# Batch 0's loads issued in one run, its tables built in waiting time, and the first odd product made in unit 5, in an FNet mixing and maxout feed-forward kernel

## The chip, the core and the metric

The kernel runs on one core of one Trainium2 chip. The metric is the device time of one execution in microseconds. The core has a matrix engine (PE, TensorE; its weight loads are listed apart as PEld), a vector engine (DVE), an activation engine (ACT), a general engine (POOL, GpSimd) and a queue engine that only issues transfers (SP). Each engine takes its own instructions strictly in the order in which the program wrote them; engines wait for one another through semaphores.

## The reference

The input `x` has 8 batches of 3072 tokens by 256 features. First comes a mixing step without weights: a discrete Fourier transform over the tokens and over the features, of which the real part is kept. Then each of the 24576 tokens goes through a feed-forward layer whose hidden value is the largest of three products:

```python
X = np.fft.fft(np.fft.fft(x, axis=1), axis=2).real      # 8 x 3072 x 256
t = X.reshape(24576, 256)
h = np.maximum(np.maximum(t @ w1, t @ w2), t @ w3)      # w1, w2, w3: 256 x 768
out = h @ w_out                                          # w_out: 768 x 256
```

Inputs and output are float32.

## The kernel before

**The mathematics.** The transform over the 3072 tokens is split as 24 x 128: stage `s` (class `Mix`, lines 440 to 456) multiplies by 24-point matrices `m24f` and `m24r`, and stage `k` (lines 460 to 476) by cosine and sine tables `tabs` with 13 rows of 128 angles, each row in three copies: sine, cosine and the sine's negative (`tab_minus`). The transform over the features is never applied to the tokens. It is multiplied into the weights once, at the start: `prep_first` and `prep_second` make `gE`, `gO`, `gD` (the features' table times w2 - w1 and w3 - w1, for the even and the odd part) and `gw` (the features' table times w1 times w_out). So the maximum becomes w1's part plus relu and maximum of two differences, and w1's part reaches the output through `gw` directly. Tokens r and 3072 - r share their even part and differ in the sign of the odd part; each token pair is therefore computed once as "plus" (`hp`) and once as "minus" (`hm`).

**The odd part once.** For one group of 128 token pairs (a slot; 12 slots to a batch), `l2_even` multiplies the even part by `gw` for two slots at a time, and ACT copies the result to `even`. `l2_odd` multiplies the odd part into a bank `po`; DVE forms `other = twice * scalar - po` (line 543) from it, where `twice` is a table that is made once from `gw`; POOL adds `other` to the even part (line 546) to get the minus half. The hidden products (`l2_hidden`, line 516: six for plus, six for minus) accumulate onto `po`. DVE adds `po` and the even lines into `ot` (line 570). The minus half is scattered to its rows by POOL (line 573), the plus half is stored by SP. There are two `po` banks, so a slot's odd product waits until `ot` of the slot two before it has been read from its bank.

**Order of the work.** The order is written out by hand; each engine's queue is the order of the program. A batch has three blocks of six units, 18 units in all. A unit on PE is four matmuls of 512 columns (`unit_plus`, lines 491 and 492), two for the minus side of the unit before (`unit_minus`, line 499), then some steps of a queue of hidden products of the block before (`l2_some`), then what a table `plan` has at that unit. The plan holds the next batch's transform (`s0` to `s6`, `k0` to `k5`), the loads of later batches on SP, and the casts (`turn_chunk`) by which POOL turns a loaded chunk of 32 or 33 rows into bf16, once forward (line 148) and once reversed (line 151). For batch 1 the casts stand in units 0, 2, 5 and 8 of batch 0, and stage `s0`, which reads all four chunks, in unit 10. Each PSUM bank of a unit is freed when ACT has taken its relu (`stmp`, line 505) and DVE its maximum (`hp` or `hm`, line 506) of the plus and the minus side; there are two banks of each kind, so unit n + 2 waits for both sides of unit n.

**The start.** POOL issues batch 0's first 112 rows as sixteen transfers that cast to bf16 on the way (`load_rows`, line 102), with iotas for the tables between them, and after them the weights. The weights' first half also releases batch 1's loads on SP. DVE makes the angles of the tables, ACT their sines; the angle rows 0 to 6 come first, then 7 to 12, then the 24-point matrices. PE runs 27 warming matmuls on `tab` (line 666), which read rows 0 and 1 of it and so wait for `tab_minus(0, 7)`. Then come batch 0's stages: `s0` to `s6`, half of the first weight product, `k0`, `k1`, the other half. In the units of block 0 follow four more pieces of `prep_first`, three of `prep_second` for `g1t` (line 404, one `pst` bank each), `gw` (line 413), and `twice` (line 422). Batch 0's rows 0 to 111 are turned and copied by ACT and DVE themselves (`turn_rows`, `lay_rows`, lines 133 and 325).

In block 1 of batch 0 the odd products are started ahead of time only when the even lines exist already. Otherwise `l2_block` makes them where they are needed:

```python
if (b, slot) not in odd:
    if (b, slot) not in lines:
        yield from l2_even(b, slot)
    l2_odd(b, slot)
```

Of the kernel before, what the change touches and what calls it, by code (L numbers as in the profile page):

```python
# [33 lines left out]
def kernel(  # L34
# [51 lines left out]
    mark = consts.tile([1, 1], FP32, tag="mark")  # L86
    two_row = consts.tile([128, 128], BF16, tag="two_row")
    sgn = consts.tile([128, 1], FP32, tag="sgn")
    dif = consts.tile([128, 1], FP32, tag="dif")
    twice = consts.tile([128, 256], FP32, tag="twice")  # L90
    t_mid = consts.tile([128, 2, B], BF16, tag="t_mid")
# [70 lines left out]
    def iota(t, pattern, base=0, cm=0):  # L162
        nc.gpsimd.iota(t, pattern, base=base, channel_multiplier=cm,
                       allow_small_or_imprecise_dtypes=True)
# [11 lines left out]
    iota(j128, [[1, 128]])  # L176
    i13 = gen.tile([128, 13], FP32, tag="i13")
    iota(i13, [[1, 13]])
# [3 lines left out]
    iota(jm24[:, 13:24], [[-1, 11]], base=-1)  # L182
    iota(jm24[:, 24:37], [[1, 13]])
    iota(jm24[:, 37:48], [[1, 11]], base=1)
    g24 = gen.tile([96, 5], FP32, tag="g24")
    iota(g24, [[24, 5]])
# [3 lines left out]
    iota(dvec[:, 2:4], [[64, 2]], base=32)  # L190
    load_rows(nc.gpsimd, x0v[:, 64:96, :], 0, 64, 96)
    load_rows(nc.gpsimd, x0v[:, 96:112, :], 0, 96, 112)

    first_half = None
    for jh in range(2):
# [4 lines left out]
        if jh == 0:  # L200
# [15 lines left out]
    for (name, value) in (("half_pi", 0.5 * math.pi), ("rnd", ROUND), ("n24", -24.0)):  # L216
# [4 lines left out]
    nc.vector.memset(two_row, 0.0)  # L221
    nc.vector.memset(two_row[0:1], 2.0)
    nc.vector.memset(gw[:, 512:513], 0.0)
    nc.vector.memset(gw[0:1, 512:513], 1.0)
    nc.vector.memset(m0f[:, 50:52], 0.0)
    nc.vector.memset(m0r[:, 50:52], 0.0)
    half = gen.tile([128, 256], FP32, tag="half")
    nc.vector.memset(half[:, 0:128], 64.0)
    nc.vector.memset(half[:, 128:256], 0.0)
# [4 lines left out]
    nc.vector.tensor_scalar(out=pi13, in0=i13, scalar1=pidx, scalar2=1.0 / 3072.0,  # L234
                            op0=ALU.mult, op1=ALU.mult)

    w = gen.tile([128, 13 * 128], FP32, tag="w")
    v = gen.tile([128, 13 * 128], FP32, tag="v")
    q = gen.tile([128, 13 * 128], FP32, tag="q")
    turn = 2.0 * math.pi  # L240

    def tab_angles(r0, r1):
        cs = slice(r0 * 128, r1 * 128)
        n = r1 - r0
        nc.vector.scalar_tensor_tensor(
            out=v[:, cs].rearrange("p (r j) -> p r j", j=128),
            in0=j128.unsqueeze(1).to_broadcast([128, n, 128]), scalar=p128,
            in1=pi13[:, r0:r1].unsqueeze(2).to_broadcast([128, n, 128]),
            op0=ALU.mult, op1=ALU.add)
        nc.vector.tensor_scalar(out=q[:, cs], in0=v[:, cs], scalar1=ROUND, scalar2=None,  # L250
                                op0=ALU.add)
        nc.vector.scalar_tensor_tensor(out=w[:, cs], in0=q[:, cs], scalar=-ROUND, in1=v[:, cs],
                                       op0=ALU.add, op1=ALU.subtract)

    def tab_sines(r0, r1):
        cs = slice(r0 * 128, r1 * 128)
        wr = w[:, cs].rearrange("p (r j) -> p r j", j=128)
        nc.scalar.activation(out=tabs[:, r0:r1, 0, :], in_=wr, func=AX.Sin, scale=-turn)
        nc.scalar.activation(out=w[:, cs], in_=w[:, cs], func=AX.Abs)
        nc.scalar.activation(out=tabs[:, r0:r1, 1, :], in_=wr, func=AX.Sin, scale=-turn,  # L260
                             bias=consts_of["half_pi"])

# [55 lines left out]
    def turn_rows(copy, r0, n, d0, d1):  # L318
        reverse(copy, xr0, x0_first[:, r0 * 64:(r0 + n) * 64], r0, n, d0, d1)
# [4 lines left out]
    def lay_rows(copy, xs, r0, n, d0=0, d1=33):  # L324
        copy(out=xn0[:, d0:d1, r0:r0 + n],
             in_=bass.AP(xs.tensor, xs.offset + d0, [xs.ap[0], [1, d1 - d0], [64, n]]))

    def bf_rows(r0, n):
# [8 lines left out]
    lay_rows(on_act, bf_rows(0, 32), 0, 32)  # L337
    lay_rows(on_dve, bf_rows(32, 32), 32, 32)

    turns = gen.tile([128, 256], BF16, tag="turns")  # L340
    nc.vector.memset(turns, 1.0)
    nc.vector.memset(turns.rearrange("p (q two g) -> p q two g", two=2, g=4)[:, :, 1, :], -1.0)
    vm = gen.tile([128, 256], FP32, tag="vm")
    qm = gen.tile([128, 256], FP32, tag="qm")
    nc.vector.scalar_tensor_tensor(
        out=vm.rearrange("p (k c) -> p k c", c=128),
        in0=dvec.unsqueeze(1).to_broadcast([128, 2, 128]), scalar=pidx,
        in1=half.rearrange("p (k c) -> p k c", c=128), op0=ALU.mult, op1=ALU.add)
    nc.vector.tensor_scalar(out=vm[:, 128:129], in0=pidx, scalar1=128.0, scalar2=64.0,
                            op0=ALU.mult, op1=ALU.add)  # L350
    nc.vector.tensor_scalar(out=qm, in0=vm, scalar1=256.0 * ROUND, scalar2=None, op0=ALU.add)
    nc.vector.scalar_tensor_tensor(out=vm, in0=qm, scalar=-256.0 * ROUND, in1=vm,
                                   op0=ALU.add, op1=ALU.subtract)
    nc.scalar.activation(out=md[0], in_=vm, func=AX.Sin, scale=float(-2.0 * math.pi / 256.0))
    turn_rows(on_act, 63, 32, 54, 65)
    turn_rows(on_dve, 63, 32, 32, 54)
    lay_rows(on_dve, bf_rows(64, 32), 64, 32)
    nc.vector.tensor_tensor(out=md[1], in0=md[0], in1=turns, op=ALU.mult)
    nc.vector.tensor_scalar(out=nmd_all, in0=md_all, scalar1=-1.0, scalar2=None, op0=ALU.mult)
    for (copy, a, b, c) in ((on_act, 49, 64, 17), (on_dve, 32, 49, 0)):  # L360
        turn_rows(copy, 95, 17, a, b)
        if copy is on_act:
            turn_rows(copy, 95, 16, 64, 65)
        lay_rows(copy, bf_rows(96, 16), 96, 16, c, c + 17 - c // 17)
    tab_minus(7, 13)
    nc.vector.tensor_scalar(out=sgn, in0=pidx, scalar1=0.0, scalar2=None, op0=ALU.is_equal)
# [297 lines left out]
    warm = ps_s.tile([128, 512], FP32, name="warm", tag="ps")  # L664
    for _ in range(27):
        nc.tensor.matmul(warm, tab[:, 0:128], tab[:, 0:512], start=True, stop=True)  # L666
    m = Mix(0)
    x0f = (lambda d: xn0[:, d, 0:128], rows_back(xr0))
    for k in range(7):
        m.s(k, x0f, pool=ps_s if k % 4 else ps_f,  # L670
            evict=nc.vector.tensor_copy if k in (1, 3, 5) else nc.scalar.copy)
    slots = [ps_s, ps_s, ps_f, ps_f]
    first = prep_first(0, lambda: slots.pop(0).tile([128, 512], FP32, name="psg", tag="ps"))
# [152 lines left out]
```

## Time and profile before

| | us |
|---|---|
| median of three runs | 422.15 (422.12 to 422.38) |
| the profiled execution | 422.23 |
| its span, first to last instruction | 420.3 |

Shares of the span: PE 94%, PEld 64%, DVE 74%, ACT 63%, POOL 76%. The granted clock of TensorE is recorded as full throughout. DMA moves 51.90 MB, a mean of 123 GB/s.

How to read the rows. In a row of the timeline the first number is the start in microseconds from the start of the span, the second is the time it took (for a row with x4, from the first start to the last end), then engine, line, operation, output from input and shapes. In brackets stands the idle time of the engine just before, and what ended it. A row of the waits reads "engine, what it was about to do, from whom it waited: microseconds in total, times, longest". Matmuls overlap in the rows: a 512-column matmul is shown with about 0.38 us, but the next one starts 0.22 us after it; a 256-column one has 0.27 us and 0.11 us.

### The profile page before, as it was taken

The numbers are of one execution on the slowest core, as the hardware profiler recorded it, in microseconds if no ns is written. First come the engines' busy times: TensorE is split into PE (matmuls) and PEld (weight loads), VectorE is DVE, ScalarE is ACT, GpSimd is POOL, SyncE is SP. The second block draws the span as 40 slices with busy tenths as digits, with TensorE's granted clock in tenths as the row PEclk, the third lists the DMA queues.
The fourth block names the chain that finished last, engine by engine and source line by source line (L and its number), as shares of the span: only waits on it lengthen the run. The fifth ranks groups of instructions, "written<-read, shape, count | busy, mean of one in ns | idle before, by whom it ended". The sixth has DMA issues, their size and how long they took to land.

```text
span 420.3 us, 9060 instructions
## 1 busy us (share of the span) xinstructions
PE 396.6 (94%) x3029; PEld 270.3 (64%) x3084; DVE 310.7 (74%) x558; ACT 263.3 (63%) x478; POOL 318.1 (76%) x431
## 2 busy tenths in 40 slices
PE   0898789999999999999999999999999999999996
PEld 0365457666776677667766676667766677666665
DVE  8868477677777877787767867787767877778884
ACT  6856546765676576656676566656676576655550
POOL 9927675999998888898887798898887844545551
PEclk9999999999999999999999999999999999999999
DMA  9999885386315863198314863177411222111314
GB/s 107 99 176 181 169 211 145 96 197 154 117 63 140 214 127 109 63 214 184 117 62 127 209 144 110 63 190 178 147 64 62 77 65 76 64 64 44 109 62 139
DMA packets 131174, 51.90 MB, mean 123 GB/s; under 512 B 113073, under 2 KB 128184, under 8 KB 131128
## 3 DMA queue, kind: packets, MB, share of 16 engines
q1 hardware_dynamic: 105408, 35.93, 35.6%
q0 software_dynamic: 24784, 15.08, 16.6%
q8 instruction: 24, 0.39, 0.4%
q10 hardware_dynamic: 936, 0.33, 0.3%
q14 instruction: 22, 0.18, 0.2%
HBM read 29.02 MB, written 25.17 MB: 129 GB/s over the span
## 4 chain that ended last, share of the span: by engine, by line
PE 91%; DVE 2%; ACT 2%; issue 2%; POOL 2%; DMA 1%; DVEq 0%; ACTq 0%; POOLq 0%
PE po L516 29%; PE pse L491 16%; PE pse L499 14%; PE pse L492 12%; PE ps L445 3%; PE ps L447 3%; PE po L540 3%; PE ps L473 2%; PE ps L471 2%; PE pl L529 2%; PE warm L666 2%; PE psg L385 1%; ACT stmp L505 1%; DMA out_dram<-ot 1%; POOL x L151 1%
## 5 line engine op out<-in xcount | busy, mean ns | idle before, releaser
L505 ACT ACTIVATE stmp<-pse 128x512 bf16<-128x512 f32 x288 | 171.4, 600 | 44.9 <-PE pse L492 29.0
L506 DVE TENSOR_TENSOR hp<-pse,stmp 128x512 bf16<-128x512 f32 x144 | 99.5, 691 | 92.5 <-ACT stmp L505 63.7
L573 POOL DMA_INDIRECT out_dram<-ot,rows_m x92 | 103.2, 1121 | 55.7 <-DVE ot L570 43.9
L491 PE MATMUL pse<-t,gE 128*128 128x512 bf16 x287 | 108.8, 379 | 2.2 <-ACT t L475 0.2
L506 DVE TENSOR_TENSOR hm<-pse,stmp 128x512 bf16<-128x512 f32 x144 | 99.1, 688 | 3.7 <-ACT stmp L505 3.5
L492 PE MATMUL pse<-t,gO 128*128 128x512 bf16 x250 | 94.6, 379 | 0.1
L516 PE MATMUL po<-wout_bf,hp 128*128 128x256 bf16 x576 | 85.9, 272 | 3.9 <-DVE other L543 3.9
L516 PE MATMUL po<-wout_bf,hm 128*128 128x256 bf16 x570 | 85.6, 273 | 0.2
L546 POOL TENSOR_TENSOR even<-even,other 128x256 f32<-128x256 f32 x92 | 66.4, 722 | 25.4 <-DVE other L543 22.9
L499 PE MATMUL pse<-t,gD 128*128 128x512 bf16 x272 | 82.2, 379 | 0.7
L516 PEld LDWEIGHTS <-hp 128*128 128x128 bf16 x576 | 56.3, 98 | 21.6 <-issue 6.6
L148 POOL CAST x<-xs 96x544 bf16<-96x544 f32 (+2 forms) x52 | 60.7, 1171 | 11.0 <-DMA xs<-in_x_dram 11.0
L516 PEld LDWEIGHTS <-hm 128*128 128x128 bf16 x576 | 56.3, 98 | 16.7
L570 DVE TENSOR_TENSOR ot<-po,even 128x512 f32<-128x512 f32 x92 | 62.8, 682 | 0.5 <-POOL even L546 0.3
L151 POOL CAST x<-xs 96x544 bf16<-96x544 f32 (+5 forms) x59 | 62.5, 1069 | 0.0
L475 ACT CAST t<-ps 128x512 bf16<-128x512 f32 x47 | 27.5, 585 | 38.2 <-PE ps L473 35.3
L499 PEld LDWEIGHTS <-gD 128*128 128x128 bf16 x288 | 27.9, 98 | 32.2
L452 ACT CAST z_all<-ps 128x480 bf16<-128x480 f32 x45 | 25.1, 558 | 36.9 <-PE ps L447 35.4
L543 DVE SCALAR_TENSOR_TENSOR other<-twice,po 128x256 f32<-128x256 f32 x92 | 43.8, 476 | 0.0
L492 PEld LDWEIGHTS <-gO 128*128 128x128 bf16 x288 | 28.1, 98 | 20.4 <-issue 1.7
L491 PEld LDWEIGHTS <-gE 128*128 128x128 bf16 x288 | 28.1, 98 | 20.3 <-issue 1.6
L532 ACT COPY even<-pl 128x512 f32<-128x512 f32 x46 | 27.0, 586 | 10.3 <-PE pl L529 9.8
(157 smaller groups left out, 379.7 us busy)
## 6 DMA issues: line engine op xcount, KB each, us to landing
xs<-in_x_dram SPq DMA_DIRECT2D x84, 198.0 KB
out_dram<-ot SPq DMA_DIRECT2D x90, 128.0 KB
xs<-in_x_dram SPq DMA_DIRECT2D x28, 192.0 KB
out_dram<-ot,rows_m POOLq DMA_INDIRECT x92
x<-in_x_dram POOLq DMA_DIRECT2D x12, 96.0 KB
w_bf<-in_moe_w_dram POOLq DMA_DIRECT2D x6, 192.0 KB
out_dram<-ot SPq DMA_DIRECT2D x17, 64.0 KB
xs<-in_x_dram SPq DMA_DIRECT2D x32, 5.8 KB
```

Of the source, the lines that this page charges most:

```text
L148: nc.gpsimd.tensor_copy(v[:, d0:d1, ch * 32:ch * 32 + 32], xs[:, 0:32 * 64].rearrange("p (bb dl) -> p dl bb", dl=64)[:, d0:d1, :])
L151: reverse(lambda out, in_: nc.gpsimd.tensor_copy(out, in_), v[:, 33:66, :], xs, ch * 32, 33 if ch == 3 else 32, 32 + d0, 32 + d1)
L491: nc.tensor.matmul(pse[:, 0:n], gE[i][:, js], te, start=True, stop=False)
L492: nc.tensor.matmul(pse[:, 0:n], gO[i][:, js], to, start=False, stop=True)
L499: nc.tensor.matmul(pse, gD[i][:, js], to, start=False, stop=True, skip_group_check=True)
L505: nc.scalar.activation(out=stmp[:, 0:n], in_=pses[0][:, 0:n], func=AX.Relu)
L506: nc.vector.tensor_tensor(out=dst, in0=src3, in1=stmp[:, 0:n], op=ALU.max)
L516: nc.tensor.matmul(po, hcols(jc), wout_bf[:, jc * 256:(jc + 1) * 256], start=False, stop=(jc == NJC - 1), skip_group_check=True)
L543: nc.vector.scalar_tensor_tensor(out=other, in0=twice, scalar=po[:, 256:257], in1=po[:, 0:256], op0=ALU.mult, op1=ALU.subtract)
L546: nc.gpsimd.tensor_tensor(out=line[:, 256:512], in0=line[:, 0:256], in1=other, op=ALU.add)
L570: nc.vector.tensor_tensor(out=ot, in0=po, in1=lin, op=ALU.add)
L573: stored(nc.gpsimd.indirect_dma_start(out, bass.IndirectOffsetOnAxis(ap=rows_m[0:128 - lo, b * 12 + slot: b * 12 + slot + 1], axis=0), ot[ ...
```

## The change

- **Loads.** The sixteen x loads of POOL follow each other directly. The iotas `i13`, `jm24`, `g24` and `dvec` are gone; DVE builds these small tables from `j128` with copies and scalar operations.
- **Tables.** The angle of row r and column j was computed for every row with three passes (product plus offset, rounding, difference). Now the rounded product `step` is formed once for 128 columns, and each row group takes two passes (offset minus `step`, then a correction by one where it exceeds a half). The rows come in groups 0 to 2, 3 to 6, 7 to 9 and 10 to 12. Only the first two groups stand ahead of the 24-point matrices; the passes of the other two stand between DVE's row copies, their sines between ACT's row copies, and the last sines (rows 10 to 12) after stage `s6`. `tab_minus(7, 13)` moves behind the stages too.
- **Features' table.** `vm` is made in two operations, its rounding stands behind DVE's last row copy, the sine `md[0]` behind stage `s2`'s copy on ACT, and `md[1]` and `nmd_all` behind `s3`'s copy on DVE (a copy and a negation of halves in place of a product with `turns`).
- **Memsets.** Those of `two_row` and of a column of `gw` move from DVE's start to POOL, behind the row numbers. Those of `half` and `turns` are gone.
- **Warming.** 35 matmuls in place of 27.
- **Last rows.** Of rows 96 to 111 DVE copies 22 of 33 columns reversed and 20 of 33 forward (17 and 17 before), ACT the others.
- **Weight products.** Of `prep_second`'s pieces two stand in unit 2 (one before), the third in unit 3, `gw` in unit 4, `twice` in unit 5. Behind it in unit 5 stands `l2_first`: the even lines of slots 0 and 1 and the odd product of slot 0. The branch in `l2_block` that made odd products where they are needed is gone.

Because slots 0 and 1 then have their even lines by unit 6, the order on the other engines changes with it. On POOL it was, in units 5 to 10: chunk 2's casts, slot 0's addition, slot 0's scatter, slot 1's addition, slot 2's addition, chunk 3's casts, the scatters of slots 1 and 2, slot 3's addition. After the change it is: slot 0's addition, chunk 2's casts, slot 1's addition, slot 0's scatter, slot 2's addition, slot 1's scatter, chunk 3's casts, slot 3's addition. From block 2 of batch 0 on, the order on all engines is the same as before. Cut to its core:

```diff
-    load_rows(nc.gpsimd, x0v[:, 0:32, :], 0, 0, 32)
-    jm24 = gen.tile([96, 48], FP32, tag="jm24")
-    iota(jm24[:, 0:13], [[1, 13]])
...
-    load_rows(nc.gpsimd, x0v[:, 32:64, :], 0, 32, 64)
-    dvec = gen.tile([128, 128], FP32, tag="dvec")
-    iota(dvec.rearrange("p (dl g) -> p dl g", g=4), [[1, 32], [64, 4]])
...
+    for r0 in (0, 32, 64):
+        load_rows(nc.gpsimd, x0v[:, r0:r0 + 32, :], 0, r0, r0 + 32)
     load_rows(nc.gpsimd, x0v[:, 96:112, :], 0, 96, 112)
...
     nc.gpsimd.tensor_copy(rows_m, rows_f)
+    nc.gpsimd.memset(two_row, 0.0)
+    nc.gpsimd.memset(two_row[0:1], 2.0)
+    nc.gpsimd.memset(gw[:, 512:513], 0.0)
+    nc.gpsimd.memset(gw[0:1, 512:513], 1.0)
...
+    nc.vector.tensor_scalar(out=step, in0=j128, scalar1=p128, scalar2=None, op0=ALU.mult)
+    nc.vector.tensor_scalar(out=near, in0=step, scalar1=ROUND, scalar2=None, op0=ALU.add)
+    nc.vector.scalar_tensor_tensor(out=step, in0=near, scalar=-ROUND, in1=step,
+                                   op0=ALU.add, op1=ALU.subtract)
...
     def tab_angles(r0, r1):
...
+        nc.vector.tensor_tensor(
+            out=wr.rearrange("p (r j) -> p r j", j=128),
+            in0=pi13[:, r0:r1].unsqueeze(2).to_broadcast([128, n, 128]),
+            in1=step.unsqueeze(1).to_broadcast([128, n, 128]), op=ALU.subtract)
+        nc.vector.scalar_tensor_tensor(out=wr, in0=wr, scalar=0.5, in1=wr,
+                                       op0=ALU.is_gt, op1=ALU.subtract)
...
-    tab_angles(0, 7)
-    tab_sines(0, 7)
-    tab_angles(7, 13)
-    tab_sines(7, 13)
+    for (r0, r1) in ((0, 3), (3, 7)):
+        tab_angles(r0, r1)
+        tab_sines(r0, r1)
...
     turn_rows(on_act, 0, 31, 32, 65)
+    tab_angles(7, 10)
+    tab_angles(10, 13)
+    lay_rows(on_act, bf_rows(0, 32), 0, 32)
+    tab_sines(7, 10, (0, 1))
     turn_rows(on_dve, 31, 32, 32, 65)
...
-            if (b, slot) not in odd:
-                if (b, slot) not in lines:
-                    yield from l2_even(b, slot)
-                l2_odd(b, slot)
...
-    for _ in range(27):
+    for _ in range(35):
         nc.tensor.matmul(warm, tab[:, 0:128], tab[:, 0:512], start=True, stop=True)
...
     for k in range(7):
         m.s(k, x0f, pool=ps_s if k % 4 else ps_f,
             evict=nc.vector.tensor_copy if k in (1, 3, 5) else nc.scalar.copy)
+        if k == 2:
+            nc.scalar.activation(out=md[0], in_=vm, func=AX.Sin, scale=float(-2.0 * math.pi / 256.0))
+        if k == 3:
...
+    tab_sines(10, 13, (1, 2))
+    tab_minus(7, 13)
...
+    def l2_first():
+        for _ in l2_even(0, 0):
+            pass
+        l2_odd(0, 0)
+
     for (u, fn) in ((0, prep_some), (0, prep_some), (1, prep_some), (1, prep_some),
-                    (2, lambda: m.k(2)), (2, prep_some), (3, lambda: m.k(3)),
-                    (3, prep_some), (4, prep_some), (5, prep_some), (5, prep_some),
+                    (2, lambda: m.k(2)), (2, prep_some), (2, prep_some),
+                    (3, lambda: m.k(3)), (3, prep_some), (4, prep_some),
+                    (5, prep_some), (5, l2_first),
                     (6, lambda: m.k(4)), (7, lambda: m.k(5)), (7, m.end),
```

More of the change, by code (lines that the diff above doesn't have):

```diff
@@ L233 @@
     pi13 = gen.tile([128, 13], FP32, tag="pi13")
-    nc.vector.tensor_scalar(out=pi13, in0=i13, scalar1=pidx, scalar2=1.0 / 3072.0,
+    nc.vector.tensor_scalar(out=pi13, in0=j128[:, 0:13], scalar1=pidx, scalar2=1.0 / 3072.0,
                             op0=ALU.mult, op1=ALU.mult)
-    w = gen.tile([128, 13 * 128], FP32, tag="w")
-    v = gen.tile([128, 13 * 128], FP32, tag="v")
-    q = gen.tile([128, 13 * 128], FP32, tag="q")
+    step = gen.tile([128, 128], FP32, tag="step")
+    near = gen.tile([128, 128], FP32, tag="near")
@@ L242, in tab_angles @@
     def tab_angles(r0, r1):
-        cs = slice(r0 * 128, r1 * 128)
+        wr = rows_of(r0, r1)
         n = r1 - r0
[L245 to L251, printed above, removed]
@@ new lines, in tab_angles, with tab_sines @@
+        nc.vector.scalar_tensor_tensor(out=wr, in0=wr, scalar=0.5, in1=wr,
+                                       op0=ALU.is_gt, op1=ALU.subtract)
+    def tab_sines(r0, r1, parts=(0, 1, 2)):
+        wf = rows_of(r0, r1)
+        wr = wf.rearrange("p (r j) -> p r j", j=128)
+        if 0 in parts:
+            nc.scalar.activation(out=tabs[:, r0:r1, 0, :], in_=wr, func=AX.Sin, scale=-turn)
+        if 1 in parts:
+            nc.scalar.activation(out=wf, in_=wf, func=AX.Abs)
+        if 2 in parts:
+            nc.scalar.activation(out=tabs[:, r0:r1, 1, :], in_=wr, func=AX.Sin, scale=-turn,
+                                 bias=half_pi[:, 0:1])
@@ L265, in tab_minus @@
                                 scalar1=-1.0, scalar2=None, op0=ALU.mult)
-    tab_angles(0, 7)
-    tab_sines(0, 7)
-    tab_angles(7, 13)
-    tab_sines(7, 13)
+    for (r0, r1) in ((0, 3), (3, 7)):
+        tab_angles(r0, r1)
+        tab_sines(r0, r1)
+    jm24 = gen.tile([96, 48], FP32, tag="jm24")
+    up = j128[0:96]
+    nc.vector.tensor_copy(out=jm24.rearrange("p (k c) -> p k c", c=24)[:, :, 0:13],
+                          in_=up[:, 0:13].unsqueeze(1).to_broadcast([96, 2, 13]))
+    nc.vector.tensor_scalar(out=jm24[:, 13:24], in0=up[:, 1:12], scalar1=-1.0, scalar2=None,
+                            op0=ALU.mult)
+    nc.vector.tensor_copy(out=jm24[:, 37:48], in_=up[:, 1:12])
+    g24 = gen.tile([96, 5], FP32, tag="g24")
+    nc.vector.tensor_scalar(out=g24, in0=up[:, 0:5], scalar1=24.0, scalar2=None, op0=ALU.mult)
     s24 = gen.tile([96, 24], FP32, tag="s24")
@@ L353 @@
                                    op0=ALU.add, op1=ALU.subtract)
[L354 to L365, printed above, removed]
     nc.vector.tensor_scalar(out=sgn, in0=pidx, scalar1=0.0, scalar2=None, op0=ALU.is_equal)
@@ L671 @@
             evict=nc.vector.tensor_copy if k in (1, 3, 5) else nc.scalar.copy)
+        if k == 2:
+            nc.scalar.activation(out=md[0], in_=vm, func=AX.Sin, scale=float(-2.0 * math.pi / 256.0))
+        if k == 3:
+            halves = [t.rearrange("p (q two g) -> p two q g", two=2, g=4) for t in md]
+            nc.vector.tensor_copy(out=halves[1][:, 0], in_=halves[0][:, 0])
+            nc.vector.tensor_scalar(out=halves[1][:, 1], in0=halves[0][:, 1], scalar1=-1.0,
+                                    scalar2=None, op0=ALU.mult)
+            nc.vector.tensor_scalar(out=nmd_all, in0=md_all, scalar1=-1.0, scalar2=None, op0=ALU.mult)
+    tab_sines(10, 13, (1, 2))
+    tab_minus(7, 13)
     slots = [ps_s, ps_s, ps_f, ps_f]
```

64 lines of the change are left out of this document (29 added, 35 removed).

## The prediction

> **What bounds the kernel now.** I read the page first, then who waited for whom on PE, then the engines in order of time up to 60 us, where all the edits lie.
>
> ```profile
> PE 396.6 (94%) x3029; PEld 270.3 (64%) x3084; DVE 310.7 (74%) x558; ACT 263.3 (63%) x478; POOL 318.1 (76%) x431
> ...
> PE warm L666 <- DVE tab L264: 11.8, 1, 11.8
> PE po L516 <- DVE other L543: 3.9, 3, 1.3
> PE pst L422 <- DVE gw L418: 0.8, 1, 0.8
> ```
>
> The first line is the page's busy time, the others PE's waits over the whole span. After its first matmul PE waits for almost nothing except three times 1.3 us for the correction `other` and once 0.8 us for `gw`. So TensorE is the bound from about 60 us on, and a microsecond won on PE before that is kept to the end. The start is the other place:
>
> ```profile
> 11.75 8.72 PE L666 MATMUL warm<-tab 128*128 128x512 bf16 x27 [11.75 <-DVE tab L264]
> 20.52 0.20 PE L445 MATMUL ps<-m24f,nat 96*128 96x96 bf16 x1
> ...
> 16.82 0.15 PEld L666 LDWEIGHTS <-tab 128*128 128x128 bf16 x1 [0.28 <-issue]
> 17.25 2.73 PEld L666 LDWEIGHTS <-tab 128*128 128x128 bf16 x13 [0.27 <-issue]
> ...
> 1.50 3.62 POOL L102 DMA_DIRECT2D x<-in_x_dram  x4 [0.21 <-issue]
> 5.11 0.49 POOL L163 IOTA jm<- 96x13 f32 x4
> 5.62 3.26 POOL L102 DMA_DIRECT2D x<-in_x_dram  x4
> 8.88 0.63 POOL L163 IOTA dvec<- 128x128 f32 x2
> 9.60 7.19 POOL L102 DMA_DIRECT2D x<-in_x_dram  x8
> ...
> 19.50 0.75 ACT L133 COPY back<-x 96x255 bf16<-96x255 bf16 x2 [1.52 <-DMA x<-in_x_dram]
> ...
> 19.52 0.41 DVE L133 COPY back<-x 96x289 bf16<-96x289 bf16 x1 [0.24 <-DMA x<-in_x_dram]
> 19.85 0.53 DVE L325 COPY nat<-x 96x272 bf16<-96x272 bf16 x1
> ```
>
> In order: PE's 27 warming matmuls and the first real one; their weight loads; POOL's queue of sixteen x loads with iotas between them; the waits for the last landing and the copies behind it. Two things end together near 20.5: the copies (DVE at 19.85 + 0.53 = 20.38) and the warming row (11.75 + 8.72 = 20.47). Either alone would hold the start.
>
> **The change, part by part.**
>
> *Loads in one run.* Gone between loads are the iotas of `jm24`, `g24` and `dvec` (gaps 5.62 - 5.11 = 0.51 and 9.60 - 8.88 = 0.72; `jm24` and `g24` fill the first), ahead of them that of `i13` (about 0.15, the excess of the first load's start over what `pidx` and `j128` need). The last load is issued about 1.37 earlier. The bounds of what that brings in landing are 0 (the transfers, not the issue, set the rate) and 1.37; I take 1.37, since ACT and DVE stood waiting for the landing 2.7 us after the last issue (16.79), the delay of one load rather than of a backlog. Rows land at 18.13. DVE's last pieces grow from 289 + 272 to 374 + 320 elements, 0.86 to about 1.0 us; ACT's shrink. Data for the first matmul: 19.15 + 0.14 = 19.3.
>
> *Tables in free time.*
>
> ```profile
> 2.09 1.15 DVE L245 SCALAR_TENSOR_TENSOR v<-j,p,pi 128x896 f32<-128x896 f32 x1
> ...
> 6.88 0.96 DVE L252 SCALAR_TENSOR_TENSOR w<-q,v 128x768 f32<-128x768 f32 x1
> ...
> 10.09 0.25 DVE L30 TENSOR_TENSOR v<-v,q 96x96 f32<-96x96 f32 x1
> ...
> 11.19 0.41 DVE L264 TENSOR_SCALAR tab<-tab 128x896 bf16<-128x896 bf16 x1
> ...
> 10.55 0.27 ACT L301 ACTIVATE t<-v 96x96 f32<-96x96 f32 x1
> ```
>
> The warming row waits for `tab_minus(0, 7)`, which stands behind `m24f`/`m24r`, behind ACT's sine `t24`, behind the sines of rows 7 to 13. After the change DVE does about 0.6 us of memsets less, three 128-wide steps (0.22 each), two passes of 384 and two of 512 (at 1.15 us per 896 plus overhead: 0.57 and 0.71 each, 2.6 in all) in place of six passes (2.09 to 7.79, 5.7 us), and 0.4 for tables once made by POOL. Its small chain (7.79 to 10.34) then ends near 7.9, ACT is free by 6.9, `t24` ends at 8.2, and the warming row starts at 9.2, 2.55 earlier. The passes for rows 7 to 13, `dvec` and `vm` (about 3 us on DVE, 2.4 on ACT) lie in waits for rows: by the rows' sums DVE reaches its last wait at 17.3 and ACT at 17.2, before 18.1.
>
> The row is eight longer. In the trace 13 start 0.427 apart until 17.25, the other 14 at 3.23 / 14 = 0.231. With the same 5.5 us of slow start: 9.2 + 5.5 + 22 x 0.231 = 19.8. The bounds are no slow matmul at all (9.2 + 35 x 0.231 = 17.3, data then holds at 19.3) and all slow (24.1); I take the trace's own 5.5. So the first real matmul moves from 20.52 to 19.8: a gain of 0.7.
>
> The Trainium skill (TensorE: Matmul & The Clock Gate, Part 1: The HAM clock gate) says that the fast clock comes after one busy window of 3.4 us, that the windows run free of the kernel, and that the number of slow matmuls thus varies. This trace agrees in kind: 5.5 us lies between one window and two. By that rule the row could end between 18.9 and 20.4, and the start, held by the data at 19.3 at the earliest, gains 0.1 to 1.2.
>
> *`md` behind the first stages.*
>
> ```profile
> 23.59 0.49 PE L385 MATMUL psg<-w_bf,nmd_all 128*128 128x384 bf16 x2
> ...
> 24.76 0.48 ACT L392 CAST gO<-psg 128x384 bf16<-128x384 f32 x1 [0.92 <-PE psg L385]
> ...
> 34.05 2.03 POOL L148 CAST x<-xs 96x1056 bf16<-96x1056 f32 x1 [9.95 <-DMA xs<-in_x_dram]
> ```
>
> The sine (256 columns, about 0.4) stands behind the copy of stage 2, its mirror and negation (0.2 + 0.2 + 0.29) behind stage 3 on DVE; ready 3.25 after the first matmul, where `nmd` was used at 23.59 - 20.52 = 3.07. With DVE's late `gE` I charge 0.25 (bounds 0 and 0.6). The late sines of rows 10 to 13 lie in ACT's 0.92 wait ahead of `gO`: nothing. The memsets of `two_row` and `gw` go into POOL's 9.95 us of waiting before 34.05: nothing; uncovered, the 0.4 that they took on DVE. Net at unit 0: 0.45 earlier.
>
> *Weight products a unit sooner.*
>
> ```profile
> 33.32 0.60 PE L404 MATMUL pst<-md_all,w_bf 128*128 128x256 bf16 x4
> ...
> 39.54 1.47 PE L413 MATMUL psw<-wout_bf,g1t 128*128 128x256 bf16 x12
> 41.79 0.27 PE L422 MATMUL pst<-gw,two_row 128*128 128x256 bf16 x1 [0.78 <-DVE gw L418]
> ...
> 33.52 0.58 ACT L475 CAST t<-ps 128x512 bf16<-128x512 f32 x1
> ...
> 41.05 0.69 DVE L418 CAST gw<-psw 128x512 bf16<-128x512 f32 x1 [0.21 <-PE psw L413]
> ...
> 41.77 0.47 ACT L419 ACTIVATE gw<-psw,sgn 128x256 bf16<-128x256 f32 x1 [1.66 <-DVE gw L418]
> ...
> L505 ACT ACTIVATE stmp<-pse 128x512 bf16<-128x512 f32 x288 | 171.4, 600 | 44.9 <-PE pse L492 29.0
> ```
>
> In unit 2 stage `k(2)` and two `pst` now follow each other in a pool of two banks: the second `pst` waits until ACT has emptied `k(2)` (34.10), not 33.76: a new wait of 0.39. The wait of 0.93 for `gw` (40.86 to 41.79) goes, as unit 5's matmuls stand between. But ACT's queue now holds the scaled copy of `gw` ahead of unit 5's relus: it waits for DVE's `gw`, takes 0.47, and only then come two relus, 0.6 each by the page's group of them, that free unit 4's bank. By the rows' sums PE reaches unit 6 at 40.8 and finds that bank free at 41.7, the other at 42.45: a new wait of about 1.2. This part gives about nothing, 0.2 lost (bounds: 0.9 won if ACT is not late, 0.6 lost).
>
> *First odd product in unit 5.*
>
> ```profile
> 45.01 0.82 PE L516 MATMUL po<-wout_bf,hp 128*128 128x256 bf16 x6 [1.32 <-DVE other L543]
> ...
> 49.85 0.38 PE L516 MATMUL po<-wout_bf,hp 128*128 128x256 bf16 x2 [1.32 <-DVE other L543]
> ...
> 51.94 0.27 PE L540 MATMUL po<-gw,t 128*128 128x257 bf16 x1
> ...
> 58.84 0.38 PE L516 MATMUL po<-wout_bf,hp 128*128 128x256 bf16 x2 [1.31 <-DVE other L543]
> 59.06 0.21 PE L445 MATMUL ps<-m24f,x 96*128 96x96 bf16 x1
> ...
> 53.78 0.72 POOL L546 TENSOR_TENSOR even<-even,other 128x256 f32<-128x256 f32 x1 [2.15 <-DVE other L543]
> 54.45 2.02 POOL L148 CAST x<-xs 96x1056 bf16<-96x1056 f32 x1
> 56.42 2.17 POOL L151 CAST x<-xs 96x1056 bf16<-96x1056 f32 x2
> 58.76 1.03 POOL L573 DMA_INDIRECT out_dram<-ot,rows_m  x1 [0.17 <-issue]
> ```
>
> With slot 0's product in unit 5 the lines of slots 0 and 1 exist when unit 6 asks for slot 1's, so every later product is made ahead, and the three waits (about 1.4 us each with the matmuls' tails) have no place left. The first two are won in full: slot 2's product, at 51.94, comes at 0.45 - 0.2 + 2.75 = 3.0 earlier, counting two more hidden matmuls done by then (0.22). It stands at 49.15.
>
> The third is not, for POOL. Stage s0 of batch 1 (59.06) needs POOL's casts of chunk 3, which ended at 58.59, so before the change the wait on PE covered them. POOL is moved too: its order was slot 2's addition, chunk 3, slot 1's scatter; now it is slot 2's addition, slot 1's scatter, chunk 3. The scatter takes 1.03 and waits for DVE's `ot`, which stands behind DVE's `other` for slot 2. From slot 2's product: `other` ends 1.85 later (1.7 before: product at 51.94, POOL's addition at 53.78), at 51.0, `ot` at 51.65, the scatter at 52.95, the casts (54.45 to 58.59, 4.14) at 57.1, s0 at 57.3. PE alone would be there at 55.2 (0.35 of waiting for slot 3's bank included), so it stands for 2.1 us.
>
> On SP the store of slot 1 moves ahead of batch 2's last chunk; that chunk's buffer is free only after POOL's casts of chunk 3, and it is wanted units later: nothing.
>
> **The sum.** s0 moves from 59.06 to 57.3, 1.8 earlier, with 0.22 of work done beyond: 2.0 won. From there PE is the bound and keeps it. The profiled execution took 422.23 with a span of 420.3, near the runs' median of 422.15. 422.23 - 2.0 = 420.2.
>
> **The rivals.**
>
> *POOL is not last:* the casts are ready when PE comes, and the gain is 59.06 - 55.2 + 0.22 = 4.1, so 418.1. For it: spans on POOL are rough. Against: chunk 3 would have to start 2.1 us sooner than the queue lets it.
>
> *The start brings nothing:* the slow stretch of the warming row lasts longer, the first matmul starts at 20.4 (in the sentence on the skill, the late end), and all behind comes 0.6 later: 420.8. With the landing no earlier at all, near 421. For it: the row has eight more matmuls and its length is not fixed by the program. Against: it starts 2.55 earlier.
>
> *Slower:* slot 1's scatter is late and holds chunk 3 behind it. Its `ot` needs POOL's addition for slot 1, which now stands behind the 4 us of chunk 2. If `ot` ends after 53.9 instead of 51.65, s0 comes later than before (59.28 counting the extra work); 3.1 us late gives 423.1. For it: DVE and ACT run close behind PE in units 2 to 6. Against: chunk 2's casts end near 48.2, over 2 us before that addition is needed.
>
> **How the numbers follow.** Forecast 0.62; POOL not last 0.14; start without gain 0.17; slower 0.07. A change under 0.2% (0.84 us) cannot be told from none, so faster means below 421.3: the first two, and most of the third, give 0.86; the third's rest, with part of the fourth, 0.09; slower 0.05. The range takes in the third case up to 421.4 and the second nearly: 418.3 to 421.4.
>
> **What would show it.** The warming row starts near 9.2 and the first stage at 19.3 to 20.4; no wait of PE for `other` remains; a wait at unit 6 for ACT or DVE; and at s0 PE waits for POOL's cast of `x`, about 2 us. If s0 shows no wait, I have mis-sized POOL; if the first stage begins after 20.5, the start.

## The result

| | median us | lowest to highest | executions |
|---|---|---|---|
| before | 422.17 | 422.12 to 422.38 | 5 |
| changed | 418.51 | 418.00 to 419.98 | 5 |

The ratio is 0.9922, with a 95% interval of 0.9898 to 0.9946: the changed kernel is 3.7 us faster. The five executions of the changed kernel fall into two groups, three at 418.0 to 418.5 and two near 420, which before did not show; the profiled one is of the second group (419.98, span 418.2), and what parts them is the first thing to read below.

PE's waits in the changed kernel, over the whole span:

```profile
PE warm L668 <- DVE tab L258: 8.9, 1, 8.9
PE ps L453 <- POOL x L153: 1.7, 1, 1.7
PE pse L497 <- ACT stmp L511: 0.5, 1, 0.5
PE psg L391 <- DMA w_bf<-in_moe_w_dram: 0.3, 1, 0.3
...
PE ps L451 <- ACT nat L327: 0.3, 1, 0.3
PE pse L497 <- DVE hm L512: 0.2, 1, 0.2
```

The three waits of 1.3 us for `other` and the one of 0.8 for `gw` are gone. New are one of 1.7 for POOL's cast of `x` and small ones for ACT, for DVE's `hm` and for the weights' landing.

The start, in order of time: PE, its weight loads, POOL's loads, and the last copies on ACT and DVE:

```profile
8.86 9.42 PE L668 MATMUL warm<-tab 128*128 128x512 bf16 x35 [8.86 <-DVE tab L258]
18.58 0.20 PE L451 MATMUL ps<-m24f,nat 96*128 96x96 bf16 x1 [0.29 <-ACT nat L327]
...
12.23 5.55 PEld L668 LDWEIGHTS <-tab 128*128 128x128 bf16 x26 [0.28 <-issue]
...
1.48 13.96 POOL L104 DMA_DIRECT2D x<-in_x_dram  x16 [0.29 <-issue]
...
17.44 0.61 ACT L135 COPY back<-x 96x170 bf16<-96x170 bf16 x2
17.95 0.55 ACT L327 COPY nat<-x 96x208 bf16<-96x208 bf16 x1
...
17.46 0.48 DVE L135 COPY back<-x 96x374 bf16<-96x374 bf16 x1
17.86 0.57 DVE L327 COPY nat<-x 96x320 bf16<-96x320 bf16 x1
```

The first real matmul comes at 18.58, 1.94 earlier than before (20.52). The sixteen loads are issued by 15.44 (16.79 before), rows 96 to 111 are copied from 17.44 on (19.50 before); neither ACT nor DVE shows a wait for their landing, so they had landed by then. The warming row ended at 18.28, so here the copies, done at 18.43 on DVE and 18.50 on ACT, were last; PE's 0.29 us of idle time is put down to ACT's.

Units 2 to 10, PE, then ACT, then POOL:

```profile
31.84 0.60 PE L410 MATMUL pst<-md_all,w_bf 128*128 128x256 bf16 x4
32.68 0.60 PE L410 MATMUL pst<-md_all,w_bf 128*128 128x256 bf16 x4 [0.24 <-ACT t L481]
39.61 0.27 PE L546 MATMUL po<-gw,t 128*128 128x257 bf16 x1
40.37 0.38 PE L497 MATMUL pse<-t,gE 128*128 128x512 bf16 x1 [0.48 <-ACT stmp L511]
41.20 0.38 PE L497 MATMUL pse<-t,gE 128*128 128x512 bf16 x1 [0.24 <-DVE hm L512]
47.88 0.27 PE L546 MATMUL po<-gw,t 128*128 128x257 bf16 x1
53.77 0.22 PE L451 MATMUL ps<-m24f,x 96*128 96x96 bf16 x1
55.67 0.22 PE L453 MATMUL ps<-m24r,x 96*128 96x96 bf16 x1 [1.69 <-POOL x L153]
...
38.87 0.47 ACT L425 ACTIVATE gw<-psw,sgn 128x256 bf16<-128x256 f32 x1 [1.66 <-DVE gw L424]
39.24 1.08 ACT L511 ACTIVATE stmp<-pse 128x512 bf16<-128x512 f32 x2
...
49.73 0.72 POOL L552 TENSOR_TENSOR even<-even,other 128x256 f32<-128x256 f32 x1 [0.49 <-DVE other L549]
50.62 1.02 POOL L575 DMA_INDIRECT out_dram<-ot,rows_m  x1 [0.16 <-issue]
51.68 2.03 POOL L150 CAST x<-xs 96x1056 bf16<-96x1056 f32 x1
53.65 2.13 POOL L153 CAST x<-xs 96x1056 bf16<-96x1056 f32 x2
```

Stage s0 of batch 1 begins at 53.77 with the forward half, and goes on with the reversed half only at 55.67, as POOL's casts of chunk 3 end. They stand behind slot 1's scatter (50.62) and begin at 51.68.

What parts the two groups of executions is seen in stretches of 2 us of the profiled execution; the columns are the stretch and its length, then the busy time and number of instructions of PE, PEld, DVE, ACT and POOL, then the granted clock of TensorE, the busy share of DMA and GB/s:

```profile
54.00:56.00 2.00, 0.33 (x8) 0.34 (x9) 0.52 (x1) 0.01 (x1) 2.00 (x3) 1.00 0.93 197
56.00:58.00 2.00, 2.00 (x13) 0.81 (x10) 0.57 (x1) 1.27 (x3) 1.56 (x3) 0.68 0.94 212
58.00:60.00 2.00, 2.00 (x12) 1.40 (x11) 1.21 (x3) 0.38 (x1) 0.35 (x1) 0.50 0.93 219
60.00:62.00 2.00, 1.95 (x19) 1.26 (x19) 0.96 (x2) 1.34 (x3) 1.19 (x2) 0.97 0.96 234
```

PE is nearly idle in the first stretch, and then its clock is at a half until just after 60. The executions near 420 have a mean clock of 0.996 over the span, those near 418 have 1.0. So the row shows 1.7 us of idle time at s0, and the executions near 420 lose about as much again behind it.

### The profile page after: what moved, and what is told of

Same layout as the page of the kernel before. It is cut to its first block, busy times and chain, and to the rows that moved or that the text cites. A ratio compares the mean times of both kernels' runs of the same rounds, so it can differ in the third digit from the quotient of the medians.

```text
span 418.2 us, 9081 instructions
## 1 busy us (share of the span) xinstructions
PE 399.0 (95%) x3037; PEld 271.4 (65%) x3092; DVE 310.2 (74%) x563; ACT 264.3 (63%) x484; POOL 317.9 (76%) x427
## 4 chain that ended last, share of the span: by engine, by line
PE 88%; POOL 6%; issue 2%; DMA 2%; ACT 1%; DVE 1%; POOLq 0%; ACTq 0%
PE po L522 29%; PE pse L497 16%; PE pse L505 14%; PE pse L498 12%; POOL x L104 3%; PE po L546 3%; PE ps L479 3%; PE ps L477 2%; PE ps L453 2%; PE ps L451 2%; PE pl L535 2%; PE psg L391 1%; DMA w_bf<-in_moe_w_dram 1%; POOL x L153 1%; DMA out_dram<-ot 1%
## 5 line engine op out<-in xcount | busy, mean ns | idle before, releaser
L511 ACT ACTIVATE stmp<-pse 128x512 bf16<-128x512 f32 x288 | 171.5, 600 | 45.3 <-PE pse L498 34.1
L522 PEld LDWEIGHTS <-hm 128*128 128x128 bf16 x576 | 56.7, 98 | 16.9
```

Source lines behind the costliest of these rows:

```text
L511: nc.scalar.activation(out=stmp[:, 0:n], in_=pses[0][:, 0:n], func=AX.Relu)
L522: nc.tensor.matmul(po, hcols(jc), wout_bf[:, jc * 256:(jc + 1) * 256], start=False, stop=(jc == NJC - 1), skip_group_check=True)
```

## The experiments

### The later part alone, and the start alone

The first kernel is the one before with only the plan of units 2 to 5 new and the branch gone; the second is the changed one with the old plan and the branch. The first one's edit, cut to its core:

```diff
-                    (2, lambda: m.k(2)), (2, prep_some), (3, lambda: m.k(3)),
-                    (3, prep_some), (4, prep_some), (5, prep_some), (5, prep_some),
+                    (2, lambda: m.k(2)), (2, prep_some), (2, prep_some),
+                    (3, lambda: m.k(3)), (3, prep_some), (4, prep_some),
+                    (5, prep_some), (5, l2_first),
...
-            if (b, slot) not in odd:
-                if (b, slot) not in lines:
-                    yield from l2_even(b, slot)
-                l2_odd(b, slot)
```

> The kernel before with only the later part of the change: weight products a unit sooner, first odd product in unit 5, the branch in l2_block gone; loads, tables and the 27 warming matmuls as before. Theory (in units 5 to 10 POOL's casts of chunk 3 set stage s0, whatever PE wins ahead of them): the first real matmul stays at 20.5; slot 2's product comes about 2.6 us earlier than 51.94; chunk 3's casts begin 3.8 us behind it, as in the changed kernel (47.88 to 51.68), so near 53.1, and s0 near 57.3 instead of 59.06 with a wait of PE for POOL of 1.5 to 2 us: 420.2, 2.0 less than before. Rival (PE sets s0): all three waits for `other` and the wait for `gw` are won, 4 us, 418.1.

Measured: 420.19 (twelve executions, 419.69 to 422.02), beside 422.14 for the kernel before on the same chip; ratio 0.996 (0.9946 to 0.9975). Seven executions lie at 419.7 to 420.3, five near 421.7 with a clock of 0.996. PE and POOL in its profile:

```profile
20.43 0.20 PE L445 MATMUL ps<-m24f,nat 96*128 96x96 bf16 x1
55.35 0.22 PE L445 MATMUL ps<-m24f,x 96*128 96x96 bf16 x1 [0.20 <-POOL x L148]
57.26 0.22 PE L447 MATMUL ps<-m24r,x 96*128 96x96 bf16 x1 [1.69 <-POOL x L151]
...
53.29 2.01 POOL L148 CAST x<-xs 96x1056 bf16<-96x1056 f32 x1
```

Chunk 3's casts begin at 53.29 and s0 goes on at 57.26, against 53.1 and 57.3 expected. The rival's 418.1 did not come.

> The changed kernel with the old plan of weight products and odd products (branch in l2_block back): only the loads, the tables and the warming row are new. Theory: the first real matmul at 18.6 as in the changed kernel (1.9 earlier), 0.3 to 0.5 lost again for the weights' landing and the table md, the three 1.3 us waits for `other` and the 0.8 for `gw` all present: 420.6, 1.5 less than before, and with the units-only kernel's gain it adds up to the whole 3.7. Rival (the start only moves the waits: batch 1's loads or POOL hold the units): under 0.5 less, 421.7 or more.

Measured: 420.39 (420.04 to 421.27), 1.75 less than before; ratio 0.9958 (0.9943 to 0.9973). PE's waits:

```profile
PE po L522 <- DVE other L549: 3.9, 3, 1.3
PE pst L428 <- DVE gw L424: 0.8, 1, 0.8
```

The old waits are all present and the start's gain is kept to the end. The two parts, 1.95 and 1.75, add up to 3.70 against the 3.66 of the whole change. Each of these numbers is known only to 0.6 to 1.0 us, so that they agree so closely is chance, but no large disturbance of one part by the other shows, though POOL holds s0 in one of them. POOL's queue there moves with the start: slot 2's product comes at 49.27 with the later part alone and at 47.88 in the changed kernel, and chunk 3's casts begin 4.0 and 3.8 us behind it.

### Chunk 3 ahead of the scatter

```diff
-                    (5, lambda: turn_chunk(1, 2)), (8, lambda: turn_chunk(1, 3))):
+                    (5, lambda: turn_chunk(1, 2)), (7, lambda: turn_chunk(1, 3))):
```

> The changed kernel with chunk 3's casts planned in unit 7 instead of 8, so that POOL takes them ahead of slot 2's addition and slot 1's scatter. Theory (the 1.9 us wait at s0 is POOL's order and nothing else): casts begin near 49.3, end near 53.4, s0 at 53.8 with no wait, and no stretch of half clock behind it: 416.4, 2.1 less than the changed kernel's median 418.5, all executions within 0.5. Rival 1 (chunk 3's transfer is late): the casts begin at a wait for DMA and s0 moves by less than 1 us, 417.6 or more. Rival 2 (the wait moves): slot 2's addition now waits behind the casts, `ot` of slot 2 is late and a later odd product waits for its bank about as long, 418 to 418.5.

Measured: 416.22 (415.97 to 416.76), ratio 0.9853 to before (0.9832 to 0.9874), 2.3 below the changed kernel. POOL and PE:

```profile
48.51 1.11 POOL L575 DMA_INDIRECT out_dram<-ot,rows_m  x1 [0.19 <-issue]
49.67 2.06 POOL L150 CAST x<-xs 96x1056 bf16<-96x1056 f32 x1
51.66 2.18 POOL L153 CAST x<-xs 96x1056 bf16<-96x1056 f32 x2
53.81 0.72 POOL L552 TENSOR_TENSOR even<-even,other 128x256 f32<-128x256 f32 x1
...
54.10 0.21 PE L451 MATMUL ps<-m24f,x 96*128 96x96 bf16 x1
54.15 0.20 PE L453 MATMUL ps<-m24r,x 96*128 96x96 bf16 x1
```

Both halves of s0 follow each other without a wait, although the first real matmul of this execution came at 19.35, later than in the changed kernel's. The casts begin straight behind slot 0's scatter, with no wait for DMA, so the chunk had landed. PE's longest wait behind the start is 0.5 us, so the wait did not move to another place either, and neither rival holds. Beside the three executions of the changed kernel whose clock did not fall (median 418.17) the gain is 1.95 us: this one number in the plan is worth about as much as either part of the change.

### PE kept busy at s0

```diff
+    def fill():
+        warm2 = ps_f.tile([128, 512], FP32, name="warm2", tag="ps")
+        for _ in range(9):
+            nc.tensor.matmul(warm2, tab[:, 0:128], tab[:, 0:512], start=True, stop=True)
+
+    at(0, 10, fill)
```

> The changed kernel with nine matmuls of 512 columns on the table, whose result nobody reads, in unit 10 ahead of stage s0: 9 x 0.216 = 1.9 us of work for PE in the place where it waits for POOL. Theory (half the executions run at half clock for 3.4 us after the wait at s0 because PE stood idle; the work done is the same): s0 stays where it was, the granted clock stays 1.0, all executions are like the faster ones of the changed kernel, 418.0 to 418.5, none near 420. Rival (the clock falls for another reason, such as the load on DMA at that time): some executions still near 420 with a clock below 1.

Measured: 418.79 (418.08 to 418.87), five executions, none with a clock below 0.999. The stretches behind s0:

```profile
54.00:56.00 2.00, 2.00 (x12) 0.84 (x9) 0.88 (x2) 0.36 (x1) 2.00 (x3) 1.00 0.94 239
56.00:58.00 2.00, 2.00 (x20) 1.21 (x19) 0.25 (x1) 1.32 (x3) 1.83 (x4) 1.00 0.83 175
```

Nine matmuls that compute nothing take the place of the wait, and the group near 420 is gone. Three of the five lie at 418.8, above the 418.5 expected; in the profiled one the first real matmul came at 19.27 instead of 18.58, which accounts for as much. That five executions show no half clock could be chance if it comes in two of five; together with the 22 executions of the five runs with chunk 3 early and no more than 0.5 us of waiting ahead of the first stage in the profile, none of which has a mean clock below 0.998, the wait at s0 is what brings it.

### Fewer warming matmuls

The changed kernel with 27 in place of 35:

> The changed kernel with 27 warming matmuls instead of 35. Theory (rows 96 to 111 set the start at 18.6, the warming row only has to reach up to it): the row ends near 16.5, PE then idles 2 us, the first real matmul stays at 18.6; the time is that of the changed kernel, 418.5, or up to 1.7 more if the clock falls in the idle stretch and the first stages run at half rate. Rival (the row sets the start): the first real matmul comes at 16.6 to 17.5 and the time falls by over 1 us, 417.3 or less.

Measured: 418.38 (417.77 to 423.22): five executions at 417.8 to 418.4, four at 421.1 to 423.2 with a clock of 0.992 or 0.988. PE's waits, and two stretches of a profile of the second kind:

```profile
PE ps L451 <- DVE nat L327: 1.7, 1, 1.7
PE ps L453 <- POOL x L153: 1.7, 1, 1.7
```

```profile
20.00:21.00 1.00, 1.00 (x23) 1.00 (x20) 0.65 (x2) 0.71 (x3) 0.91 (x3) 0.75 1.11 154
21.00:22.00 1.00, 1.00 (x16) 1.00 (x14) 0.97 (x4) 0.50 (x2) 0.78 (x3) 0.50 1.25 163
```

PE waited 1.7 us for the rows' copies, so the first matmul (18.95) is not earlier: the rows set it, and the rival falls. And in this profile the clock falls behind this wait too, at 20.5, and again behind the wait at s0, so that the execution loses twice; a mean of 0.992 is two such stretches, 0.988 three.

### The run of loads undone

On the kernel with chunk 3 early, iotas are put back between POOL's loads:

```diff
+    iota(pad[:, 0:13], [[1, 13]])
     load_rows(nc.gpsimd, x0v[:, 0:32, :], 0, 0, 32)
+    for n in (13, 11, 13, 11, 5):
+        iota(pad[0:96, 0:n], [[1, n]])
     load_rows(nc.gpsimd, x0v[:, 32:64, :], 0, 32, 64)
+    iota(pad.rearrange("p (dl g) -> p dl g", g=4), [[1, 32], [64, 4]])
+    iota(pad[:, 2:4], [[64, 2]], base=32)
     load_rows(nc.gpsimd, x0v[:, 64:96, :], 0, 64, 96)
```

> The kernel with chunk 3 early, and iotas like those of the kernel before put back between POOL's loads, into a tile that nobody reads: only the run of loads is undone. Theory (the issue on POOL sets the landing of rows 96 to 111): the last landing goes from 17.4 to 18.8 or later, the first real matmul to about 19.9, weights and batch 1's chunks 1.4 us later too; 0.5 to 1.4 us lost, 416.8 to 417.6, the less where the warming row runs long in any case. Rival (the transfers set it): landing and time unchanged, 416.2.

Measured: 417.80 (417.75 to 417.86), 1.58 above chunk 3 early. PE and POOL:

```profile
9.02 9.64 PE L675 MATMUL warm<-tab 128*128 128x512 bf16 x35 [9.02 <-DVE tab L265]
20.40 0.20 PE L458 MATMUL ps<-m24f,nat 96*128 96x96 bf16 x1 [1.73 <-DVE nat L334]
...
10.18 6.85 POOL L104 DMA_DIRECT2D x<-in_x_dram  x8
...
17.43 0.82 DVE L135 COPY back<-x 96x704 bf16<-96x704 bf16 x1 [1.43 <-DMA x<-in_x_dram]
```

The warming row starts at 9.02 (8.86 in the changed kernel), and PE still waits until 20.40, where the kernel before began (20.52). So of the start's 1.75 us most comes from the run of loads; the tables and the earlier warming row make room for it, as in the kernel before the row alone held PE until 20.47. The loss is more than the 0.5 to 1.4 expected, but the gaps came out longer than the old ones (the second half of the loads starts at 10.18 here and at 9.60 before, and ends at 17.03 and at 16.79), so 1.58 is an upper figure; with these 0.2 to 0.6 us taken off, an estimate is 1.0 to 1.3. Nor is it the last rows alone that set the start, as the theory had it: the last wait for a load in DVE's queue is the one of 1.43 at 17.43, for rows 64 to 95, and from there on DVE's copies follow each other. No execution showed a half clock here, though PE waited 1.7 us; the last section comes back to this.

### The products a unit sooner, undone

```diff
-                    (2, lambda: m.k(2)), (2, prep_some), (2, prep_some),
+                    (2, lambda: m.k(2)), (2, prep_some),
                     (3, lambda: m.k(3)), (3, prep_some), (4, prep_some),
-                    (5, prep_some), (5, l2_first),
+                    (5, prep_some), (5, prep_some), (5, l2_first),
```

> The kernel with chunk 3 early, and the weight products in the units of the kernel before (one pst in units 2, 3 and 4, gw and twice in unit 5), the first odd product still behind them in unit 5. Theory (the earlier products won nothing: the wait of 0.9 us for gw was traded for waits at unit 2 and unit 6): the wait for gw is back with 0.8 us, the waits at unit 2 (0.24) and unit 6 (0.9) are gone, the time is within 0.4 us of 416.2. Rival (they won their 0.9 us): 417.1.

Measured: 416.39 (416.17 to 416.56) against 416.22. Its waits:

```profile
PE pst L428 <- DVE gw L424: 0.8, 1, 0.8
PE ps L451 <- DVE nat L327: 0.4, 1, 0.4
...
PE pl L535 <- ACT gw L425: 0.2, 1, 0.2
```

The wait for `gw` is back, those at unit 2 and unit 6 are gone, and the time is the same within what these runs can tell. Of the later part of the change the whole gain is the first odd product in unit 5; the earlier weight products won nothing.

### The sign copy out of ACT's way

On the kernel with chunk 3 early:

```diff
-        nc.scalar.activation(out=gw[:, 514:770], in_=psw[:, 256:512], func=AX.Copy, scale=sgn)
...
+    at(0, 13, lambda: nc.scalar.activation(out=gw[:, 514:770], in_=gw[:, 256:512],
+                                           func=AX.Copy, scale=sgn))
```

> The kernel with chunk 3 early, and the scaled copy of gw (ACT, 0.47 us, read by the last batch alone) moved from unit 4 to unit 13, taken there from gw itself. Theory (PE's 0.9 us at unit 6 come from ACT's relus that stand behind that copy): the waits of PE at unit 6 for ACT and DVE fall from about 0.9 to 0.4 or less and s0 comes 0.4 to 0.5 earlier, 415.8 against 416.2. Rival (DVE's gw itself is what the relus' maxima wait for): waits and time unchanged, 416.2.

Measured: 415.50 (415.08 to 415.86), ratio 0.9841 (0.9827 to 0.9854); in a later run of the same kernel 415.94 (415.54 to 416.26). PE at unit 6:

```profile
39.46 0.27 PE L545 MATMUL po<-gw,t 128*128 128x257 bf16 x1
39.76 0.38 PE L496 MATMUL pse<-t,gE 128*128 128x512 bf16 x1
40.49 0.38 PE L496 MATMUL pse<-t,gE 128*128 128x512 bf16 x1
```

From the end of slot 0's product (39.46 + 0.11) the first pair waits 0.19 and the second 0.30 (40.49 - 39.76 less two steps of 0.215), 0.49 together. In the changed kernel it was 0.65 and 0.40. The copy stood in ACT's queue ahead of the relus, as the prediction had it, and what is left is DVE's. The time is 0.7 below chunk 3 early in one run and 0.3 in the other, and the two differ by 0.4 between themselves, so the rows show this gain more clearly than the times do.

### The start once more

The same kernel with 31 warming matmuls in place of 35, and with 35 again beside it:

> The kernel with chunk 3 early and the sign copy late, with 31 warming matmuls instead of 35. Theory (the rows' landing sets the start near 18.6 where the slow stretch of the row is short, the row's own end up to 19.5 where it is long): four fast matmuls less take 0.9 us off the row's end, so executions with a long slow stretch start up to 0.8 earlier and the others are unchanged; 0.2 to 0.5 below the same kernel with 35, about 415.2, and no execution with a clock below 0.99, the idle time ahead of the first stage being under 1 us. Rival (the idle time lets the clock fall, as with 27): some executions 2 us and more longer.

> The same with 35 warming matmuls, beside it on the same chip, as the measure for it: 415.5 again, within 0.5.

Measured: 415.33 (415.03 to 416.02) with 31 and 415.94 (415.54 to 416.26) with 35; the ratios to before are 0.9842 (0.9828 to 0.9855) and 0.985 (0.9835 to 0.9865). The direction is as expected and no clock fell, but the intervals overlap: not settled. The two profiles show what was meant: with 35 the copies were done at 18.27 and the row held the first matmul until 19.18, with 31 the row was through first and the copies let PE start at 18.45; but the slow stretch of the row was also shorter there, 5.0 us against 5.5. Either beats both the kernel before and the changed one, by 6.3 to 6.9 and 2.6 to 3.2 us.

## Why the prediction was right, and where it was off

The direction held, and so did the mechanism of every part but the start; 418.51 lies in the range, but 1.7 us below the 420.2 forecast, a gain of 3.66 where 2.0 was summed. One term of the sum was mis-sized. That the median lies in the range is partly luck: the range's low end is 418.3, two of the five executions (418.00 and 418.17) lie below it, and so does the median of the three whose clock did not fall, 418.17. Only the two that lost 1.7 us in a way that the forecast did not have lift it to 418.51.

- **The start: mis-sized.** The sum took 0.7 us, then 0.45 net; the start alone measured 1.75. Two numbers in it were off in the same direction. The landing was put at 18.13, the old delay of 2.7 us behind the last issue; the rows were there by 17.44, at most 2.0 behind it (with the start alone ACT waited for them until 17.42, 2.0 behind the last issue). And the slow stretch of the warming row was taken over from the one profile of before, 5.5 us, when here it was 3.4 (8.86 to 12.23, eight matmuls), so that in this profile the copies set the start and not the row, which the sum had as the last to end. The sentence on the Trainium skill's rule had the better range for the row's end, 18.9 to 20.4, and even that lies late, one reason being that the row started at 8.86, not 9.2. That the stretch varies is plain from the other runs: 5.9 us with chunk 3 early (8.86 to 14.79), where the copies were done at 19.12 and the row let the first matmul start at 19.35.
- **`md`: in place of 0.25 for the table, 0.32 for the weights.** PE waited for `w_bf` to land, as the start had overtaken it.
- **Unit 2 and unit 6: as said.** The second `pst` starts 0.40 late (0.39 said), unit 6 loses 1.05 (1.2 said), and the products late measured the sum of the trade at nothing.
- **The first two waits for `other` won in full: as said.** Slot 2's product came at 47.88 instead of 49.15; the 1.27 is the start's error carried on.
- **POOL at s0: as said.** The order slot 1's scatter, then chunk 3, costs PE 1.7 us of idle time in the profile (2.1 said); the move of chunk 3 shows it by taking it away, and with it 1.95 us of the time.
- **Not foreseen: the clock behind that wait.** The forecast priced the wait as idle time alone.

Of the rivals, POOL not last fell: the wait is in the profiles of the changed kernel and of the later part alone. The start without gain did not come; nearest to it is the profile with 35 warming matmuls in the last experiment, where the row's long slow stretch took 0.8 us (copies done at 18.27, first matmul at 19.18). The slower one fell too: `ot` of slot 1 was in time, and slot 1's scatter began at 50.62.

## What to carry to other kernels

When a wait of the bounding engine is removed, look for the work on other queues that the wait had been covering, and where it now stands in its queue: here one scatter ahead of one cast took back 2 us, and moving the cast by one unit in the plan gave about as much as either half of the change. A wait for one engine that is removed by moving work into another engine's queue (the sign copy ahead of ACT's relus) can come back from there at about the same size (0.78 us before, 1.05 at unit 6 after); a copy that only the last batch reads belongs where that queue is free. And a term that rests on one profile of something that varies between executions, such as the slow stretch at the start, is worth a look at its spread before it is put into a sum.

## What the runs showed of the hardware

- **TensorE's clock fell to a half behind a wait of 1.7 us.** It happened in two of five executions of the changed kernel, five of twelve with the later part alone, four of nine with 27 warming matmuls, in each of the profiled ones behind a wait of 1.7 us; it lasted 3.4 us (56.7 to 60.1 in the changed kernel) and cost about 1.7 us. It came not in the wait but 0.9 to 1.6 us after PE had work again. The waits of 1.3 us in the kernel before did not bring it in the five executions of the result (of 21 later ones one took 424.26, with a mean clock of 0.996; it has no profile), and with the loads' run undone a wait of 1.7 at the start did not in four. The Trainium skill (TensorE: Matmul & The Clock Gate, Part 1: The HAM clock gate) puts the fall behind at least one idle window of 3.4 us; here less than 2 us without a matmul was enough, so the measurement decides. That it comes in some executions only agrees with that section's windows that run free of the kernel.
- **When it falls fits a fixed step of 3.41 us.** In the profile with 27 warming matmuls the clock falls at 20.50, is back at 23.91, falls at 58.05 and is back at 61.46: one step, ten steps (34.1 us) and one step. Two steps ahead of 20.50, between 13.5 and 13.8, the slow stretch of the first matmuls ends; in the changed kernel and with the later part alone the fall, too, lies whole steps behind the end of that stretch (13 and 12). Counted off in these steps, the step ahead of each of the four profiled falls has the whole wait in it, and PE is busy for 1.5 to 1.7 us of its 3.41. With the loads' run undone a step ends inside the wait, which is so shared between two, each with PE busy for over 2.1 us, and the clock stays; in the kernel before, with its waits of 1.3 us, the least busy step has 1.9, and in every other profile without a fall 2.0 or more. So whether a wait of 1.7 us costs its double depends on where it falls in the steps, as far as these profiles go: this was read off afterwards, and no run moved a wait on purpose.
- **The slow stretch of the first matmuls varied.** In the kernels with the new start and 35 warming matmuls it was 3.4 us in one profile, 5.5 in another, 5.9 in a third. It moved the start by about 0.8 us where the row was the last to end (in the last experiment with 35 the copies were done at 18.27 and the first matmul came at 19.18; in the changed kernel it followed the copies by 0.08), and may be a good part of the spread between executions of the faster kernels, which no run separates. The granted clock does not show it: it reads 1.00 from 9 to 12 us in the changed kernel's profile, where the row's weight loads follow each other at 0.43 us, and at 0.22 later.
